# Opening the block of engine programs without GpSimd's closing drain

## The chip, the cores and the metric

The kernel runs on one core of one Trainium2 chip. The core has five engines, each with a program of its own: TensorE (PE, with its weight loads shown as PEld), VectorE (DVE), ScalarE (ACT), GpSimd (POOL) and SyncE (SP). The metric is the time of one execution in microseconds (us) as the device reports it. One execution is also recorded by a profiler; its page gives a span, from the first recorded instruction of the program to the end of the last one, and a time for the same execution, which is a little more than the span because it takes in what runs around the program.

## The reference

Two independent layers read different inputs, and their outputs are laid side by side in the last dimension (2048 rows, 512 + 512 columns, bfloat16).

```python
# A: attention, 32 heads of 16, over 2048 positions
qkv = (x @ wqkv)                         # split into q, k, v per head
p = softmax(q @ k.T * 16 ** -0.5)
a = (p @ v) @ wo
# B: gated long convolution, per channel
kv = shift_conv(k, shift_k) * v          # 4 taps
y = causal_conv(kv, ssm_k) + kv * ssm_D  # 2048 taps; written with FFTs
b = q * y
out = concatenate([a, b], axis=-1)
```

## The kernel before

The kernel is written as five lists of instructions, one for each engine. While the lists are made, a planner in Python keeps a clock for each engine and decides by its estimates which piece of work is put next on which engine. Nothing of that planner remains at run time: each instruction has at most a few semaphore waits before it and raises its engine's semaphore after it (`Eng.op` and `Eng.run`).

Attention is cut into 32 groups (a block of 128 feature columns, a block of 512 queries, and the even or the odd heads in it), and each group into blocks of 128 keys by 512 queries of one head. A step makes scores of several blocks on TensorE (line 829), takes their exponential on ScalarE, two or three PSUM banks at a time (line 856), or for some blocks in four passes on VectorE (lines 892, 918, 923, 927), and multiplies the result with V on TensorE (line 966). The output projection with `wo` (line 1141) follows for each 128 rows. Its result is copied out of PSUM by VectorE into `OUTA` (line 1149, `op_out`), and GpSimd starts the store of it to the output. The long convolution is done as matrix products with shifted copies of the filter (line 1236). These copies are read from a scratch tensor in memory by transfers that SyncE starts, and the work is fitted into the gaps of attention on TensorE.

Every transfer is made by one helper, `dma`, so that all of them carry line 369 in the profile. GpSimd starts the ones that rearrange queries (`QT<-QS`), that load and store the rows of `QN` for the second layer, the load of `wo`, and the stores of `OUTA`. SyncE starts nearly all others, and ScalarE three. Each transfer raises a semaphore when it lands.

The end is written out by hand. The last 128 rows of the projection are copied out in two halves at once, by ScalarE (line 1570) and VectorE (line 1568), into a free part of `QT`, and ScalarE and SyncE each start the store of one half (`d_outE`). Then SyncE waits for the landing of every store of the output, those that GpSimd started among them:

```python
for ds in d_outA + d_outB + [d_outE]:
    sp.op(lambda e, ds=ds: e.wait_ge(ds.sem, ds.n), inc=False)   # line 1573
```

After that the lists are put out inside one block, `with nc.Block() as block:` (line 1575): `pool.run`, `sp.run`, `pe.run`, `act.run` and `dve.run`. When the block closes, each engine gets a DRAIN, which holds the engine until its older instructions are complete, and then all engines meet in a barrier made of two semaphores, 96 and 97 in this program. The DRAINs of TensorE, VectorE, ScalarE and SyncE raise semaphore 96. GpSimd does its own DRAIN, then waits for semaphore 96, and raises semaphore 97, on which the other four wait. All of these carry line 1575 in the profile. The same form of barrier, with line 1611, stands in front of the program, before any transfer.

Of the kernel before, what the change touches and what calls it, by code (L numbers as in the profile page):

```python
# [274 lines left out]
def bass_concat_heads__mha_block__ssm_conv_h3__prompt_kernel(  # L275
# [1296 lines left out]
    for ds in d_outA + d_outB + [d_outE]:  # L1572
        sp.op(lambda e, ds=ds: e.wait_ge(ds.sem, ds.n), inc=False)

    with nc.Block() as block:
        @block.gpsimd
        def _(e):
            pool.run(e)

        @block.sync  # L1580
        def _(e):
            sp.run(e)

        @block.tensor
        def _(e):
            pe.run(e)

        @block.scalar
        def _(e):
            act.run(e)  # L1590

        @block.vector
        def _(e):
            dve.run(e)
# [31 lines left out]
```

## Time and profile before

| | us |
|---|---|
| median of 3 runs | 752.24 (751.03 to 752.8) |
| the profiled execution, its own time | 749.93 |
| its span | 748.2 |
| busy: ACT, PE, DVE, POOL | 724.6, 701.8, 701.3, 98.6 |

The profiled execution's time is 1.73 us over its span, and 2.31 us below the median of the runs. The clock granted to TensorE was 0.997 of full speed over the span.

Rows are read like this. In the view of a source line, each row is an engine and an operation with its count, then the shortest, median and longest duration in ns, then the start of the first and of the last one in us from the start of the span. An engine's name with a q behind it (POOLq, SPq) stands for that engine's sequencer: what it does there is not counted as busy. In the timeline a row begins with the start and the summed time in us, and ends with the idle time before it in brackets, with what ended it. In the view of stretches, each stretch has its length and then the busy time of each engine with its count of instructions.

### The profile page before, as it was taken

The page shows a single profiled execution, that of the slowest core. Times are in us where ns is not written, and L with a number is a line of the kernel's source. Part 1 is how long each engine was busy: PE and PEld are TensorE (multiplying, and loading weights), DVE is VectorE, ACT ScalarE, POOL GpSimd, SP SyncE. Part 2 cuts the span into 40 slices and gives each one's busy share as a digit, 9 for nine tenths or more (in the row PEclk, how much of TensorE's full clock was granted, in tenths as well). Part 3 has the DMA queues.
Part 4 walks back from the last instruction along what each step waited for, and adds up shares of the span by engine and source line. Part 5 has one row for each costly group of instructions (what it writes and reads, how often), then busy time and mean ns, then how long its engine had stood idle before and what let it go on. Part 6 is the DMA issues. An engine that isn't in the chain of part 4 may idle for free.

```text
span 748.2 us, 32527 instructions
## 1 busy us (share of the span) xinstructions
PE 701.8 (94%) x14696; PEld 315.0 (42%) x14696; DVE 701.3 (94%) x1437; ACT 724.6 (97%) x690; POOL 98.6 (13%) x172
## 2 busy tenths in 40 slices
PE   8999899999999999999999999999899999999996
PEld 3334244445443454444444444444343443434353
DVE  3999999999999999999899998999999997989993
ACT  6999999999999999999999999999899999999995
POOL 7202102020202002020021302020011201210000
PEclk9999999999999999999999999999999999999999
DMA  9698757777785777776677578666787575766110
GB/s 217 185 238 285 226 181 226 254 251 239 237 256 180 256 278 234 259 231 225 171 235 227 179 233 274 207 208 222 257 294 254 179 238 187 246 223 224 55 31 30
DMA packets 73720, 161.48 MB, mean 216 GB/s; under 512 B 34064, under 2 KB 37776, under 8 KB 73200
## 3 DMA queue, kind: packets, MB, share of 16 engines
q1 hardware_dynamic: 66400, 150.43, 62.8%
q0 software_dynamic: 5984, 8.66, 3.9%
q8 instruction: 116, 1.90, 1.0%
q10 hardware_dynamic: 1200, 0.33, 0.2%
q14 instruction: 20, 0.16, 0.1%
HBM read 142.61 MB, written 6.42 MB: 199 GB/s over the span
## 4 chain that ended last, share of the span: by engine, by line
ACT 59%; DVE 23%; PE 13%; DMA 3%; issue 1%; POOLq 0%; POOL 0%; SPq 0%
ACT PT L856 59%; DVE PTD L892 10%; PE PS L829 4%; DVE PTD L923 4%; PE PS L966 4%; DVE PTD L918 2%; DVE PTD L927 2%; DMA WR<-kz_scratch 2%; PE PS L1236 2%; PE PS L516 1%; DVE DT L1064 1%; PE PS L1493 1%; DMA xT<-in_A_x_dram 1%; DVE KV L604 1%; DVE VA L621 0%
## 5 line engine op out<-in xcount | busy, mean ns | idle before, releaser
L856 ACT ACTIVATE PT<-PS 128x1024 bf16<-128x1024 f32 (+2 forms) x686 | 722.3, 1287 | 8.6 <-PE PS L829 8.3
L892 DVE TENSOR_SCALAR PTD<-PS 128x512 uint16<-128x512 f32 x464 | 312.1, 687 | 15.0 <-PE PS L829 14.2
L829 PE MATMUL PS<-QT,KTo 32*128 32x512 bf16 (+2 forms) x2248 | 271.0, 366 | 24.4 <-ACT PT L856 14.5
L1236 PE MATMUL PS<-WR,KV 128*24 128x128 bf16 (+8 forms) x8192 | 180.8, 220 | 2.6 <-DMA WR<-kz_scratch 1.9
L966 PE MATMUL PS<-PT,VA 128*32 128x512 bf16 (+2 forms) x1748 | 180.4, 367 | 2.7 <-DVE VA L621 1.3
L1236 PEld LDWEIGHTS PS<-WR,KV 128*32 128x32 bf16 (+7 forms) x8192 | 134.5, 95 | 59.0 <-issue 33.7
L923 DVE TENSOR_TENSOR PTD<-PTD 128x1024 f16<-128x1024 f16 x232 | 156.5, 686 | 0.3
L966 PE MATMUL PS<-PTD,VA 128*32 128x512 f16 (+1 forms) x1000 | 151.8, 368 | 0.5 <-DVE PTD L927 0.4
L829 PEld LDWEIGHTS PS<-QT,KTo 32*128 32x128 bf16 x2248 | 71.2, 91 | 192.2 <-ACT PT L856 138.7
L369 POOL DMA_DIRECT2D QT<-QS x120 | 61.1, 516 | 396.1 <-DVE QS L582 372.2
L927 DVE TENSOR_SCALAR PTD<-PTD 128x1024 uint16<-128x1024 uint16 x232 | 96.5, 422 | 0.3
L918 DVE TENSOR_SCALAR PTD<-PTD 128x1024 uint16<-128x1024 uint16 x232 | 93.6, 422 | 0.3
L966 PEld LDWEIGHTS PS<-PT,VA 128*32 128x32 bf16 x1748 | 45.6, 94 | 88.2 <-issue 69.3
L966 PEld LDWEIGHTS PS<-PTD,VA 128*32 128x32 bf16 x1000 | 38.7, 95 | 12.8 <-issue 2.2
L1487 PE MATMUL PS<-IDN,ZW 128*32 128x512 bf16 (+3 forms) x178 | 42.6, 307 | 0.3 <-DVE DT L1064 0.2
L369 POOL DMA_DIRECT2D out_dram<-OUTA x15 | 8.8, 584 | 107.1 <-DVE OUTA L1149 107.1
L1064 DVE STREAM_TRANSPOSE DT<-PS 128x512 f32<-128x512 f32 x31 | 22.1, 714 | 0.4 <-PE PS L966 0.2
L570 PE MATMUL PS<-WKV,xT 128*128 128x128 bf16 x256 | 19.3, 220 | 1.1 <-DVE KTo L591 0.5
L516 PE MATMUL PS<-xT,WQ 128*32 128x512 bf16 x240 | 18.3, 384 | 1.2 <-DVE DT L1064 0.8
L516 PE MATMUL PS<-xT,WKV 128*32 128x512 bf16 (+1 forms) x256 | 18.4, 381 | 1.0 <-DVE QN L1271 0.5
L1487 PEld LDWEIGHTS PS<-IDN,ZW 128*32 128x32 bf16 x178 | 13.2, 95 | 12.7 <-issue 8.4
L570 PEld LDWEIGHTS PS<-WKV,xT 128*128 128x128 bf16 x256 | 14.4, 98 | 8.8 <-issue 3.8
(72 smaller groups left out, 250.0 us busy)
## 6 DMA issues: line engine op xcount, KB each, us to landing
WR<-kz_scratch SPq DMA_DIRECT2D x256, 512.0 KB, 5.4
KV<-KV SPq DMA_DIRECT2D x16, 256.0 KB, 5.6
kz_scratch<-WR SPq DMA_DIRECT2D x1, 2176.0 KB, 8.3
QN<-in_B_q_dram POOLq DMA_DIRECT2D x8, 256.0 KB, 5.0
out_dram<-QN POOLq DMA_DIRECT2D x8, 256.0 KB, 2.9
QT<-QS POOLq DMA_DIRECT2D x120, 16.0 KB, 4.3
out_dram<-OUTA POOLq DMA_DIRECT2D x15, 128.0 KB, 2.5
QN<-in_B_ssm_k_dram SPq DMA_DIRECT2D x1, 1024.0 KB, 8.2
```

The lines of the kernel that those rows point to most:

```text
L369: f(outp, inp).then_inc(dsem.sem, 16)
L516: ins = e.matmul(dst[g:g + 32], lhsT=w[:, g:g + 32], rhs=rhs, tile_position=(0, g), **kw)
L570: ins = e.matmul(PS[:, bank, 128 * j:128 * j + 128], lhsT=xT[:, dc, (4 * sc + j) * 128:(4 * sc + j + 1) * 128], rhs=WV[:, dc, o * 128:(o + ...
L829: ins = e.matmul(PS[:, bank, i * w:i * w + w], lhsT=KTo[32 * s:32 * s + 32, OF[n_] % 2, kt * 128:(kt + 1) * 128], rhs=QT[32 * s:32 * s + 3 ...
L856: h = act.op(lambda e: e.activation(PT[:, p0:p0 + n, :], src, ACT.Exp, scale=EXP_SCALE, bias=EXP_BIAS), [h, free], us=(0.065 + 0.4257 * n, ...
L892: h_f = urgent(lambda e: e.tensor_scalar(fix_u, PS[:, bank, :], FIX_ADD, FIX_HI, ALU.add, ALU.min), [h, h_ptd.get(i - R_PTD)], slack=S_FX)
L918: st["h"] = dve.op(lambda e: e.tensor_scalar(mant_u, fix_u, MANT, HALF_BITS, ALU.bitwise_and, ALU.bitwise_or), [st["h"]], us=us)
L923: st["h"] = dve.op(lambda e: e.tensor_tensor(mant, fix, mant, ALU.mult), [st["h"]], us=us)
L927: h = dve.op(lambda e: e.tensor_scalar(fix_u, fix_u, OCTAVE, ONE_MORE, ALU.bitwise_and, ALU.bitwise_or), [st["h"]], us=us)
L966: ins = e.matmul(dst, lhsT=w, rhs=rhs, start=first, stop=last, tile_position=(0, 32 * s))
L1236: ins = e.matmul(PS[32 * g:32 * g + 2 * ((30 - d) // 2 + 1), BGB, 128 * kk:128 * kk + w], lhsT=kv, rhs=WR[:, r + g, S - 64 * d - 128:S - 6 ...
L1487: pe.op(lambda e, s=s, k=k, rhs=rhs, bank=bank, rows=rows, c0=c0, first=first: e.matmul(PS[32 * s:32 * s + rows, bank, c0:c0 + 128 * k], l ...
```

## The change

The block is opened with an option that leaves GpSimd's DRAIN out of its closing. The other four engines still drain, and the barrier that follows is made of semaphore instructions alone: it holds GpSimd until the four have arrived, as before, but GpSimd comes to it without having drained. The five lists of instructions themselves, their waits, and the waits of SyncE for the stores are as before. Nothing that is computed changes.

```diff
     for ds in d_outA + d_outB + [d_outE]:
         sp.op(lambda e, ds=ds: e.wait_ge(ds.sem, ds.n), inc=False)
 
-    with nc.Block() as block:
+    with nc.Block(no_gpsimd_drain=True) as block:
         @block.gpsimd
         def _(e):
             pool.run(e)
```

## The prediction, made before the result was known

> **What bounds the kernel now.** I read the page first. ScalarE, TensorE and VectorE are each busy over 93% of the span, and GpSimd 13%.
>
> ```profile
> span 748.2 us, 32527 instructions
> ...
> PE 701.8 (94%) x14696; PEld 315.0 (42%) x14696; DVE 701.3 (94%) x1437; ACT 724.6 (97%) x690; POOL 98.6 (13%) x172
> ```
>
> So for most of the span the exponentials on ScalarE set the pace, with two other engines close behind. The edit touches none of that. It touches only what is recorded under line 1575, so the view that decides is the one of that source line.
>
> ```profile
> L1575 POOLq EVENT_SEMAPHORE  x2: 17/17/17, 748.0 to 748.1; - x2
> L1575 PEldq DRAIN  x1: 878/878/878, 740.6 to 740.6; - x1
> L1575 POOLq DRAIN  x1: 6514/6514/6514, 741.4 to 741.4; - x1
> L1575 DVEq DRAIN  x1: 464/464/464, 741.5 to 741.5; - x1
> L1575 ACTq DRAIN  x1: 153/153/153, 742.3 to 742.3; - x1
> L1575 SPq COMPARE_BRANCH  x1: 41/41/41, 744.0 to 744.0; - x1
> L1575 SPq DRAIN  x1: 13/13/13, 744.2 to 744.2; - x1
> L1575 SPq EVENT_SEMAPHORE  x1: 17/17/17, 748.1 to 748.1; - x1
> L1575 ACTq EVENT_SEMAPHORE  x1: 17/17/17, 748.1 to 748.1; - x1
> L1575 PEldq EVENT_SEMAPHORE  x1: 51/51/51, 748.1 to 748.1; - x1
> L1575 DVEq EVENT_SEMAPHORE  x1: 21/21/21, 748.1 to 748.1; - x1
> ```
>
> GpSimd's DRAIN takes 6514 ns, from 741.4 to about 748.0. Four engines have finished theirs at 741.5 (TensorE: 740.6 plus 0.88), 742.0 (VectorE), 742.5 (ScalarE) and 744.2 (SyncE). GpSimd's two semaphore instructions, which close the barrier, come only at 748.0 and 748.1, and all others leave right after. The second view to read is that of busy time in stretches, to see whether anything at all runs beside the long DRAIN.
>
> ```profile
> 738.00:742.00 4.00, 3.33 (x50) 1.77 (x38) 2.03 (x6) 1.35 (x3) 0.77 (x2) 1.00 0.10 35
> 742.00:744.30 2.30, 0.00 (x0) 0.00 (x0) 0.00 (x0) 0.00 (x0) 0.01 (x1) 1.00 0.36 114
> 744.30:748.20 3.90, 0.00 (x0) 0.00 (x0) 0.00 (x0) 0.00 (x0) 0.00 (x0) 0.82 0.00 0
> ```
>
> The columns after the length are PE, PEld, DVE, ACT, POOL, then clock, DMA share and GB/s. From 742.0 to 744.3 only transfers run. From 744.3 to 748.2 nothing runs: no engine, and the DMA share is 0.00. The last 3.9 us of the span are the DRAIN and the barrier alone.
>
> The third view is the timeline of the last transfers, with their times to landing and SyncE's waits.
>
> ```profile
> 741.47 0.54 POOL L369 DMA_DIRECT2D out_dram<-OUTA  x1 [3.23 <-DVE OUTA L1149]
> ...
> 741.93 0.37 ACTq L369 DMA_DIRECT2D out_dram<-QT  x1
> 741.97 0.36 SPq L369 DMA_DIRECT2D out_dram<-QT  x1
> ```
>
> ```profile
> out_dram<-OUTA POOLq DMA_DIRECT2D x2, 128.0 KB, 2.0
> out_dram<-QT ACTq DMA_DIRECT2D x1, 64.0 KB, 1.9
> out_dram<-QT SPq DMA_DIRECT2D x1, 64.0 KB, 2.0
> ```
>
> ```profile
> SPq L1575 <- PEq L1575: 3.9, 1, 3.9
> SPq L1573 <- DMA out_dram<-OUTA: 1.1, 1, 1.1
> SPq L1573 <- DMA out_dram<-QT: 0.4, 1, 0.4
> ```
>
> GpSimd's last store starts at 741.47 and lands 2.0 us later, at about 743.5; SyncE's own, at 741.97, lands at about 744.0. SyncE has waited for both before its DRAIN at 744.2, and then waits 3.9 us in the barrier. The releaser that the view names there, TensorE's DRAIN, was done at 741.5; the one that was really missing is GpSimd, by the source rows above.
>
> **The change part by part.** First, the DRAIN of 6514 ns goes. Its first part, to 744.2, lies beside the last stores and SyncE's waits and is worth nothing; that cover remains. Only what lies behind SyncE's DRAIN is on the path: from 744.2 to the barrier's first instruction on GpSimd at 748.0, 3.8 us.
>
> Second, the closing barrier stays. Its price is read from both barriers of the trace. The closing one goes from 748.0 to the end of the span at 748.2, 0.2 us. The opening one, from line 1611, is alike:
>
> ```profile
> L1611 POOLq EVENT_SEMAPHORE  x2: 17/17/17, 0.6 to 0.7; - x2
> ...
> L1611 POOLq DRAIN  x1: 179/179/179, 0.4 to 0.4; - x1
> ...
> L1611 PEldq EVENT_SEMAPHORE  x1: 51/51/51, 0.7 to 0.7; - x1
> ```
>
> It runs from 0.6 to about 0.75, again 0.2 us at the rounding of the rows. So the new program ends 0.2 us behind SyncE.
>
> Third, a plain drain followed by a semaphore instruction stands where a DRAIN raised the semaphore itself. That is one added instruction on each of four engines, 17 to 51 ns by the EVENT_SEMAPHORE rows. Only SyncE's is on the path, since the others arrive 1.7 us or more earlier. I take 0.05 us, between 0.02 (its row alone) and 0.1 (with a raise that has to travel, as between GpSimd's two rows).
>
> Fourth, what is late next: the store of the last half tile by SyncE, at 741.97 with its 2.0 us. GpSimd's store of `OUTA` is still waited for, by SyncE, so the end cannot come before about 744.0 plus the branch and DRAIN of SyncE.
>
> The new span is then 744.2 + 0.05 + 0.2 = 744.45, against 748.2: 3.75 us less, 3.7 rounded down.
>
> Fifth, the price that the trace does not show: whether something around the program has to do what the DRAIN did. The profiled execution took 749.93, which is 1.73 us more than its span, and no row tells what lies there. Two bounds follow from the rows. The least is nothing: if no one asks GpSimd again, the whole 3.7 us are gained. The most is the whole work over again. GpSimd was free for its DRAIN at 742.0 (741.47 + 0.54) and done at 748.0, so the work takes at most 6.0 us. Begun at about 744.4 instead of 742.0, it would end at 750.4, 2.4 us later than now, of which the 0.2 us of the barrier, already done, come off: a loss of 2.2 us. I take nothing. The nearest row for a drain with no transfers before it is the opening one, 179 ns, and it stands behind four small memsets that it also has to outlast; a closing sequence that only tidies up is nearer to that row than to 6 us.
>
> What makes the DRAIN long is a reason for care. Both stores of that time have landed by 744.0, yet it goes on for 4 us. Waiting for a landing is therefore not what fills it. A candidate is a charge for each transfer that GpSimd has started:
>
> ```profile
> QN<-in_B_q_dram POOLq DMA_DIRECT2D x8, 256.0 KB, 5.0
> out_dram<-QN POOLq DMA_DIRECT2D x8, 256.0 KB, 2.9
> QT<-QS POOLq DMA_DIRECT2D x120, 16.0 KB, 4.3
> out_dram<-OUTA POOLq DMA_DIRECT2D x15, 128.0 KB, 2.5
> ...
> WKV<-in_A_wo_dram POOLq DMA_DIRECT2D x1, 512.0 KB, 4.3
> ```
>
> That is 152 transfers, and 6.0 us by 152 is 39 ns for each. This is an estimate from these rows; the opening DRAIN, with no transfer behind it, fits it. If it holds, the work exists whenever someone settles those entries, and the question is only whether anyone inside the measured time does.
>
> [...]
>
> **The sum.** 749.93 - 3.7 = 746.2 for an execution like the profiled one. That execution was 2.31 us below the median of the runs, and I assume that the difference stays: 752.24 - 3.7 = 748.5, or 0.5% less.
>
> **The rivals.**
> - *Part of the work returns.* What closes the execution drops the 152 entries without waiting for each. Anything between the bounds is possible; at a quarter to a half of the 39 ns it is 1.5 to 3 us, and the time is 750.0 to 751.5, say 750.7. [...] Against it: 1.73 us around the span leave little room for long sequences.
> - *The work goes on by itself and ends when it ended.* If the DRAIN only watches something that GpSimd finishes at 748.0 in any case, and something later waits for it, the span shrinks by 3.75 us and the time by no more than the barrier's 0.2: 752.0. For it: the work starts with the last store. Against it: nothing is seen running after 744.3, though the inside of GpSimd has no rows.
> - *The work starts over later.* A drain outside the program does it all from 744.4 on. This ends on the other side: 2.2 us lost, 754.4. It decides only if that drain takes more than the 3.7 us gained; at 39 ns that is 95 of the 152 entries. For it: the estimate by count needs work and not time. Against it: someone must wait there for the same completions that the block was asked not to wait for.
> - *The option has no effect on GpSimd's DRAIN.* Then the time stays at 752.2. Against it: the option is for this DRAIN.
>
> **How the numbers follow.** Chances: the full gain 0.57; part returns 0.12; ends as before 0.10; starts over 0.18; no effect 0.03. No change is what lies within 0.2%, 1.5 us, about what a measurement of this kernel can tell. The full gain (748.5) and nearly all of the partial one (up to 750.7) are faster: 0.57 + 0.11 = 0.68. Starting over is slower: 0.18. The rest, 0.14, is the same. The three runs spread 1.2 below and 0.6 above their median, so the full gain's own range is 747.3 to 749.3. The range for 8 in 10 must also take in the partial return and the two cases near 752, and leaves out starting over: 747.0, with 0.3 us for a barrier slightly cheaper than taken, to 752.6.
>
> **What would show it.** In the new profile the row of POOLq DRAIN under line 1575 is gone, SyncE's drain stays near 744.2, GpSimd's first semaphore instruction comes at 744.3 and the span is near 744.5. The stretch with nothing in it shrinks from 3.9 to 0.3 us, and everything before 741 is alike. The span alone does not prove the gain: what counts is the execution's time over the span. At 1.7 us the full gain is right; at 3 to 5 us part of the work returned; at 5.3 us it ended as before; at over 7 us it started over. The prediction is wrong if that difference grows, or if GpSimd comes to the barrier late for another reason, such as its last store, which would show as a landing behind 744.0.

## The result, and the profile after

| | before | changed |
|---|---|---|
| median of 15 runs, us | 752.86 (750.01 to 760.29) | 746.43 (742.88 to 751.59) |
| ratio to before | | 0.9944, 95% interval 0.9922 to 0.9966 |
| the profiled execution: time, span | 749.93, 748.2 | 750.88, 749.1 |

The changed kernel is faster by 0.56%, 0.34 to 0.78%. That is 2.6 to 5.9 us of 752.86, and the 3.7 us of the forecast lie in it. The ratio is not that of the two medians, which are 6.4 us apart: single runs lie up to 10.3 us apart before and 8.7 in the changed kernel. The median of 746.43 lies 2.1 us under the forecast of 748.5 and 0.6 under its range of 747.0 to 752.6. The ratio, put on the 752.24 from which the forecast started, gives 748.0, inside the range.

The profiled execution of the changed kernel seems to contradict this: its span is 0.9 us longer than before. The closing has to be read by itself. First its source line, with engine, count, durations in ns and first and last start in us, in the changed kernel:

```profile
L1575 PEldq EVENT_SEMAPHORE  x2: 51/51/51, 746.2 to 749.0; - x2
L1575 DVEq EVENT_SEMAPHORE  x2: 21/21/21, 746.6 to 749.0; - x2
L1575 ACTq EVENT_SEMAPHORE  x2: 17/17/17, 747.1 to 749.0; - x2
L1575 SPq EVENT_SEMAPHORE  x2: 17/17/17, 748.9 to 749.0; - x2
L1575 POOLq EVENT_SEMAPHORE  x2: 17/17/17, 748.9 to 749.0; - x2
L1575 PEldq DRAIN  x1: 877/877/877, 745.2 to 745.2; - x1
L1575 DVEq DRAIN  x1: 464/464/464, 746.1 to 746.1; - x1
L1575 ACTq DRAIN  x1: 163/163/163, 746.9 to 746.9; - x1
L1575 SPq COMPARE_BRANCH  x1: 41/41/41, 748.6 to 748.6; - x1
L1575 SPq DRAIN  x1: 13/13/13, 748.8 to 748.8; - x1
```

GpSimd has no DRAIN any more. Four engines have a second semaphore instruction, the added one, and SyncE's is followed at once by GpSimd's. The span ends 0.3 us behind SyncE's DRAIN; before it was 4.0 us. Next the stretches of the end (busy time by engine, then clock, DMA share and GB/s), the last engine work, the last transfers and the barrier:

```profile
742.60:746.60 4.00, 3.31 (x50) 1.76 (x35) 2.03 (x6) 1.34 (x3) 0.77 (x2) 1.00 0.10 35
746.60:748.90 2.30, 0.00 (x0) 0.00 (x0) 0.00 (x0) 0.00 (x0) 0.00 (x0) 1.00 0.36 114
748.90:749.10 0.20, 0.00 (x0) 0.00 (x0) 0.00 (x0) 0.00 (x0) 0.00 (x0) 1.00 0.00 0
```

The first two stretches are those of before, 4.6 us later: the same 2.03 us of VectorE, and the same DMA share of 0.36 in 2.3 us in which transfers alone run. The third, with nothing in it, has shrunk from 3.9 to 0.2 us. SyncE's waits say the same:

```profile
SPq L1573 <- DMA out_dram<-OUTA: 1.1, 1, 1.1
SPq L1573 <- DMA out_dram<-QT: 0.4, 1, 0.4
SPq L1575 <- PEq L1575: 0.2, 1, 0.2
```

The wait in the barrier is 0.2 us instead of 3.9. And the anchor that both traces share, GpSimd's last store, starts 4.6 us later than before:

```profile
746.06 0.54 POOL L369 DMA_DIRECT2D out_dram<-OUTA  x1 [3.23 <-DVE OUTA L1149]
```

Starts and ends to 0.01 us, here and below, are read from the trace. From this start to the end of the span it is 749.09 - 746.06 = 3.03 us, against 748.19 - 741.47 = 6.72 before: 3.69 us less. The 4.6 us that hide it are lost long before the closing. The programs of the five engines are the same there, instruction for instruction. The exponentials' row, of before and then of the changed kernel (busy us and mean ns, then idle time before them and what ended it):

```profile
L856 ACT ACTIVATE PT<-PS 128x1024 bf16<-128x1024 f32 (+2 forms) x686 | 722.3, 1287 | 8.6 <-PE PS L829 8.3
```

```profile
L856 ACT ACTIVATE PT<-PS 128x1024 bf16<-128x1024 f32 (+2 forms) x686 | 722.6, 1290 | 13.4 <-PE PS L829 13.0
```

```profile
core 0: 749.1 us, clock 0.991
```

ScalarE worked as long as before (722.6 us against 722.3) but waited 4.8 us more, 4.7 of it for the score products of TensorE, whose granted clock was 0.991 in this execution and 0.997 in that of before. Ahead of the closing, the trace of before has one stretch of 3.41 us at half clock, at 91.4 us. The changed one has the like of it at 90.5, and three more (the clock, 0.50, stands behind the five engines):

```profile
213.36:216.77 3.41, 3.41 (x66) 1.30 (x51) 2.01 (x4) 2.01 (x2) 0.00 (x0) 0.50 0.42 91
581.99:585.40 3.41, 3.41 (x50) 1.42 (x47) 2.76 (x7) 2.59 (x4) 0.00 (x0) 0.50 0.00 0
650.26:653.67 3.41, 3.41 (x39) 0.90 (x36) 1.72 (x3) 2.05 (x2) 0.00 (x0) 0.50 0.26 89
```

TensorE is busy in all of each. Counted exponential by exponential against before, the program falls back by 2.7, 1.4 and 2.5 us across these three, and is 2.0 us ahead for the rest. That is where the 4.6 us went. In the 3.41 us just ahead of the three, TensorE was busy for only 1.49, 2.16 and 1.60; whether that is what lowers the clock was not tried. The granted clock differs between executions of one kernel, in the 15 runs of the changed one from 0.990 to 1.0: the seven with 0.998 or more have a median of 745.7, the eight below 0.996 have one of 750.2. So one profiled execution against another can't tell 3.7 us in the span; it can in the closing.

Last, the time over the span, which the forecast named as what decides: 750.88 - 749.09 = 1.79 us, before 749.93 - 748.19 = 1.74. The DRAIN's 3.7 us have not come back outside the program in this execution. Of the 15 runs of the changed kernel 13 show the same 1.7 to 1.8 us, but two show 2.2 and 2.3; none of the 46 runs of the kernel before that were made beside the experiments does.

### The profile page after: what moved, and what is told of

The parts are those of the page before. It is cut to its first block, busy times and chain, and to the rows that moved or that the text cites. A ratio compares the mean times of both kernels' runs of the same rounds, so it can differ in the third digit from the quotient of the medians.

```text
span 749.1 us, 32530 instructions
## 1 busy us (share of the span) xinstructions
PE 703.4 (94%) x14696; PEld 315.4 (42%) x14696; DVE 702.0 (94%) x1437; ACT 724.8 (97%) x690; POOL 98.7 (13%) x172
## 4 chain that ended last, share of the span: by engine, by line
ACT 60%; DVE 27%; PE 11%; issue 1%; DMA 1%; POOL 0%
ACT PT L856 60%; DVE PTD L892 11%; DVE PTD L923 5%; PE PS L829 4%; PE PS L966 4%; DVE PTD L918 3%; DVE PTD L927 3%; PE PS L1236 2%; DVE DT L1064 1%; DMA xT<-in_A_x_dram 1%; PE PS L516 1%; DVE KV L604 1%; PE PS L1493 1%; DVE OUTA L1149 1%; DVE QN L1271 0%
## 5 line engine op out<-in xcount | busy, mean ns | idle before, releaser
L856 ACT ACTIVATE PT<-PS 128x1024 bf16<-128x1024 f32 (+2 forms) x686 | 722.6, 1290 | 13.4 <-PE PS L829 13.0
L1236 PEld LDWEIGHTS PS<-WR,KV 128*32 128x32 bf16 (+7 forms) x8192 | 136.0, 95 | 58.7 <-issue 36.0
L923 DVE TENSOR_TENSOR PTD<-PTD 128x1024 f16<-128x1024 f16 x232 | 154.9, 678 | 0.3
L927 DVE TENSOR_SCALAR PTD<-PTD 128x1024 uint16<-128x1024 uint16 x232 | 94.8, 414 | 0.3
L918 DVE TENSOR_SCALAR PTD<-PTD 128x1024 uint16<-128x1024 uint16 x232 | 92.2, 415 | 0.3
L966 PEld LDWEIGHTS PS<-PTD,VA 128*32 128x32 bf16 x1000 | 38.6, 95 | 12.5 <-issue 1.6
```

The source lines that it names most:

```text
L856: h = act.op(lambda e: e.activation(PT[:, p0:p0 + n, :], src, ACT.Exp, scale=EXP_SCALE, bias=EXP_BIAS), [h, free], us=(0.065 + 0.4257 * n, ...
L918: st["h"] = dve.op(lambda e: e.tensor_scalar(mant_u, fix_u, MANT, HALF_BITS, ALU.bitwise_and, ALU.bitwise_or), [st["h"]], us=us)
L923: st["h"] = dve.op(lambda e: e.tensor_tensor(mant, fix, mant, ALU.mult), [st["h"]], us=us)
L927: h = dve.op(lambda e: e.tensor_scalar(fix_u, fix_u, OCTAVE, ONE_MORE, ALU.bitwise_and, ALU.bitwise_or), [st["h"]], us=us)
L966: ins = e.matmul(dst, lhsT=w, rhs=rhs, start=first, stop=last, tile_position=(0, 32 * s))
L1236: ins = e.matmul(PS[32 * g:32 * g + 2 * ((30 - d) // 2 + 1), BGB, 128 * kk:128 * kk + w], lhsT=kv, rhs=WR[:, r + g, S - 64 * d - 128:S - 6 ...
```

## The experiments

The theory: GpSimd's DRAIN works through the transfers that GpSimd has started and that have not been settled, at a price for each, only inside a DRAIN, and nobody else in the measured time does that work. "Settled" stands for what the DRAIN's time shows: a transfer that the next DRAIN no longer takes time for. The rivals: a fixed price behind the last landing; work that GpSimd ends by itself at its own time; a price by bytes or rows.

**One DRAIN early, the closing one kept.** The same end without the option: GpSimd drains once where it is idle anyway.

```diff
+    n_dma, ops = 0, []
+    for w, fn, sm in pool.ops:
+        ops.append((w, fn, sm))
+        n_dma += fn.__name__ == "fn"
+        if fn.__name__ == "fn" and n_dma == 149:
+            ops.append(([], lambda e: e.drain(), None))
+    pool.ops[:] = ops
     with nc.Block() as block:
```

> The closing DRAIN of GpSimd stays; one more DRAIN is put on GpSimd right after its 149th transfer, at about 716 us, ahead of 18.8 us in which it only waits. By a charge for each transfer not yet settled (39 ns), the early DRAIN takes about 5.8 us where nothing waits for GpSimd, and the closing one has 3 transfers left: it ends with the landing of the last store, some 2.1 to 2.3 us after that store was issued, ahead of SyncE. The wait of SyncE in the barrier is 0.2 us instead of 3.9 and the time is that of the changed kernel, 3.7 us (0.5%) below before. By a fixed charge behind the last landing (4 to 4.5 us whatever the count), the closing DRAIN stays at 6 to 6.5 us, the wait in the barrier at 3.8 and the time at that of before.

Ratio to before 0.9936 (0.9907 to 0.9965). The early DRAIN in its source line, and the closing one in its own, eight lines further down than before:

```profile
L1580 POOLq DRAIN  x1: 6783/6783/6783, 715.1 to 715.1; - x1
...
L1583 POOLq DRAIN  x1: 2212/2212/2212, 741.6 to 741.6; - x1
...
L1583 SPq DRAIN  x1: 13/13/13, 744.3 to 744.3; - x1
```

The long DRAIN has moved to 715, beside other work, and the closing one, with three transfers left, is over at 743.8, ahead of SyncE. It is recorded from 741.6, 0.02 us before the last store, which lands at 743.62, so its 2.2 us are that store's issue and landing: with three transfers left, this DRAIN lasted until 0.2 us behind the last landing. The gain is the same as with the option. A fixed price behind the last landing is out.

**One DRAIN late.** The changed kernel, with GpSimd waiting for all stores of the output and then draining.

```diff
+    for ds in d_outA + d_outB + [d_outE]:
+        pool.op(lambda e, ds=ds: e.wait_ge(ds.sem, ds.n), inc=False)
+    pool.op(lambda e: e.drain(), inc=False)
     with nc.Block(no_gpsimd_drain=True) as block:
```

> The changed kernel, with GpSimd made to wait for the landing of all stores of the output, as SyncE does, and then to do one DRAIN, about 2.5 us after the issue of its last store. By a charge for each transfer, worked off only inside a DRAIN, it takes the whole 152 x 39 ns = 5.9 us from there, so that the span ends 5.5 to 6 us later behind the last store than in the changed kernel, and 1.7 to 2.2 us later than before: slower than before by 0.2 to 0.3%. By work that GpSimd finishes on its own 6.5 us after its last store, it takes at most 4.0 us and the end is that of before. By a wait for landings alone it takes under 0.3 us.

Ratio 1.0023 (0.9988 to 1.0058): not faster than before, and not told apart from it by the time. The trace tells more:

```profile
L1577 POOLq DRAIN  x1: 5944/5944/5944, 746.4 to 746.4; - x1
```

GpSimd's last store started at 743.76 in this run, and all stores of the output had landed when the DRAIN began at 746.4. Most transfers were hundreds of us old, and it still takes 5.9 us. Work that ends at its own time would have been done 3.9 us after that start, 6.5 us behind the last store. The span ends 8.78 us behind the last store (752.54 - 743.76), 2.06 us more than before. So a DRAIN asked for later does all the work from there, as the third rival of the forecast had it; in the changed kernel, whose time is 1.79 us over its span, no one asks.

**32 transfers more, before the closing DRAIN.**

```diff
+    pad, d_pad = sb("PAD", [128, 256]), DmaSem(sem("d_pad"))
...
+        if fn.__name__ == "fn" and n_dma == 149:
+            for i in range(32):
+                r0, c0 = 16 * (i % 8), 64 * (i // 8)
+                d_pad.add()
+                ops.append(([], lambda e, r0=r0, c0=c0: e.dma_start(
+                    pad[r0:r0 + 16, c0:c0 + 64], QS[r0:r0 + 16, c0:c0 + 64]).then_inc(d_pad.sem, 16), None))
...
+    sp.op(lambda e: e.wait_ge(d_pad.sem, d_pad.n), inc=False)
```

> The kernel before, with 32 small transfers more on GpSimd (16 partitions x 128 bytes, into a tensor that nothing else uses), after its 149th, all landed 2 us or more before its last stores. By a charge for each transfer, the closing DRAIN is longer by 32 x 39 ns = 1.25 us: 7.7 us. By a charge by bytes or by descriptors, it is longer by less than 0.3 us; by a fixed charge it stays at 6.5 us.

```profile
L1589 POOLq DRAIN  x1: 9127/9127/9127, 744.2 to 744.2; - x1
```

9127 against 6514 ns: 2613 ns more, which is 82 ns for each of the 32. There is a price for each transfer, and it is twice my estimate. (The one time of this run, 755.29 us, is a single execution.)

**Five DRAINs along the way.** The changed kernel with a DRAIN before the 53rd, 77th, 93rd, 118th and 146th transfer of GpSimd, behind that transfer's own wait.

```diff
...
+        if fn.__name__ == "fn" and n_dma in (52, 76, 92, 117, 145):
+            ops.append((w, lambda e: e.drain(), None))
+            w = []
+        ops.append((w, fn, sm))
...
```

> The changed kernel, with five DRAINs on GpSimd, each right before a transfer and behind that transfer's wait, when everything earlier has landed long ago. Between them lie 52, 24, 16, 25 and 28 transfers. By 39 ns for each they take 2.0, 0.9, 0.6, 1.0 and 1.1 us. By a charge for each row or descriptor the fifth, with 12 stores of 128 rows among its 28, takes several times the second, whose 24 have 16 rows each. By a fixed charge all five are alike.

The same source line asked in five windows:

```profile
L1578 POOLq DRAIN  x1: 4311/4311/4311, 294.2 to 294.2; - x1
L1578 POOLq DRAIN  x1: 2002/2002/2002, 404.7 to 404.7; - x1
L1578 POOLq DRAIN  x1: 1352/1352/1352, 465.1 to 465.1; - x1
L1578 POOLq DRAIN  x1: 2083/2083/2083, 572.8 to 572.8; - x1
L1578 POOLq DRAIN  x1: 2324/2324/2324, 711.2 to 711.2; - x1
```

By 52, 24, 16, 25 and 28 transfers that is 83, 83, 84.5, 83 and 83 ns each, or 82.2 ns for each and 37 ns for the DRAIN itself. The fifth, with 12 stores of 128 KB among its 28, is as cheap for each (83.0 ns) as the second (83.4), whose 24 move 16 KB: between 16 and 128 KB no price by size shows. But 152 transfers at this price would be 12.5 us, and the late DRAIN took 5944 ns, which is 72. Where did the other 80 go?

**One DRAIN at a chosen place.** Four kernels, each the changed one with a single DRAIN as above, behind 92, 117, 129 and 141 transfers. The edit is shown against the kernel with five.

```diff
-        if fn.__name__ == "fn" and n_dma in (52, 76, 92, 117, 145):
+        if fn.__name__ == "fn" and n_dma == 92:
```

> The changed kernel, with one DRAIN on GpSimd behind 92 transfers, long after they landed. The five DRAINs lie on 82 ns for each transfer and 40 ns; by that rate the DRAIN before, with 152 transfers behind it, settled only 72, so that 80 must have been settled earlier in another way. If that happened before the 92nd, this DRAIN takes 12 x 82 ns + 40 ns = 1.0 us; if not, 92 x 82 ns + 40 ns = 7.6 us. If at most 72 are ever kept, it takes 5.9 us.

> The same, with the one DRAIN behind 117 transfers. 37 x 82 ns + 40 ns = 3.1 us if 80 have been settled by then, 117 x 82 ns + 40 ns = 9.7 us if not, 5.9 us if at most 72 are kept.

> The changed kernel, with the one DRAIN behind 129 transfers. None had been settled at 117, 80 at 149. If all are still there, 129 x 82 ns + 40 ns = 10.6 us; if 80 are gone, 49 x 82 ns + 40 ns = 4.1 us; something between, if they go a few at a time from the 118th on.

> The same behind 141 transfers: 11.6 us if all are still there, 5.1 us (61 x 82 ns + 40 ns) if 80 are gone, something between if they go a few at a time.

The DRAIN behind 92, then in one fence for each run behind 117, 129 and 141:

```profile
L1578 POOLq DRAIN  x1: 7577/7577/7577, 459.9 to 459.9; - x1
```

```profile
L1578 POOLq DRAIN  x1: 9619/9619/9619, 567.3 to 567.3; - x1
```

```profile
L1578 POOLq DRAIN  x1: 4066/4066/4066, 619.9 to 619.9; - x1
```

```profile
L1578 POOLq DRAIN  x1: 5046/5046/5046, 662.6 to 662.6; - x1
```

At 82.2 ns and 37 ns these are 92, 117, 49 and 61 transfers. All are still there at 117, and 80 are gone at 129, at 141 and at the end. They are gone at 149 as well: the early DRAIN begins under the last two issues, which end at 716.14, and from there to its end at 721.85 it is 5.71 us, 69 transfers. So the 80 go between the 118th and the 129th transfer, in one step or in a few, and without a DRAIN of the program: "only inside a DRAIN", in the theory above, does not hold for them. What sets that time was not tried. (The kernels with DRAINs along the way ran once each, 746.11 to 754.11 us, which says nothing of their speed.)

**GpSimd waits in SyncE's place.** An attempt at a still shorter closing: the waits for the stores are put on the engine that leads the barrier. Beside it ran the changed kernel once more.

```diff
     for ds in d_outA + d_outB + [d_outE]:
-        sp.op(lambda e, ds=ds: e.wait_ge(ds.sem, ds.n), inc=False)
+        pool.op(lambda e, ds=ds: e.wait_ge(ds.sem, ds.n), inc=False)
```

> The changed kernel, with the waits for the landing of the output's stores moved from SyncE to GpSimd, which leads the barrier. SyncE's branch and DRAIN behind the last landing leave the path; GpSimd has its waits, and no DRAIN, in their place. By the rows of the late DRAIN's run, GpSimd is free 0.27 us before SyncE's raise reaches it: 0.2 to 0.3 us off the end, which the trace can show and the time can't. If GpSimd takes as long as SyncE from the landing to the barrier, nothing changes.

> The changed kernel once more, beside the one above. By all theories left, 0.3 to 0.7% below before, a time 1.7 to 1.9 us over its span, and the end of the span 2.9 to 3.1 us behind the start of GpSimd's last store.

Ratios to before 0.9948 (0.9923 to 0.9973) and, for the changed kernel again, 0.9955 (0.9924 to 0.9986). From GpSimd's last store to the end of the span it is 749.51 - 746.56 = 2.95 us, against 3.02 in the repeat (747.86 - 744.84): 0.07 us instead of the 0.27 expected. The reason is in the closing's rows with GpSimd's waits:

```profile
L1575 POOLq EVENT_SEMAPHORE  x2: 17/17/17, 749.3 to 749.4; - x2
...
L1575 POOLq COMPARE_BRANCH  x1: 38/38/38, 749.1 to 749.1; - x1
```

The branch out of the list, with 0.2 us to the next instruction, which SyncE had, GpSimd now has. The time over the span, though, is 2.4 us in this profiled execution and 2.1 to 2.4 in all 12 runs, against 1.7 to 1.8 in 11 of the 12 runs of the repeat (2.4 in one). The late DRAIN's ten runs, where GpSimd ends with the same waits, show 2.2 to 2.4 as well. So 0.07 us are gained in the program and about 0.5 us lost around it. The cause of the 0.5 us is not in the rows. This is no better version.

## Why the prediction was right

- *The place* was right: only what lies behind SyncE's DRAIN was gained. The stretch with nothing in it went from 3.9 to 0.2 us and SyncE's wait in the barrier from 3.9 to 0.2. The last 4 us of work ahead of it kept their form but came 4.6 us later, for the clock, so the places named in advance, SyncE's drain near 744.2 and an end near 744.5, were met only from the common anchor on.
- *The size* was right by the trace: 3.69 us behind the common anchor, for 3.75 worked out. The barrier cost its 0.2 us, and the added semaphore instruction some 0.07: from SyncE's DRAIN to the end it is 0.30 us in the changed kernel (748.79 to 749.09) and 0.23 with the early DRAIN and the old barrier (744.335 to 744.561). The term was 0.05, between 0.02 and 0.1.
- *What is late next* was right: the end now follows the landing of SyncE's half tile, and GpSimd's store is not late.
- *The unknown price around the program* was taken as nothing: 1.74 us over the span before, 1.79 after. This was a choice more than a derivation, and lucky in part. It rested on the opening DRAIN of 179 ns, which has no transfers behind it; the late DRAIN, asked for 2.6 us behind the start of the last store, took 5.9 us, and nothing in the rows of before told that no such DRAIN would follow the block. With it fall the first rival (1.5 to 3 us return), the second (ends as before) and the fourth (no effect). A small return is left: 2.2 to 2.4 us over the span in 3 of the 27 runs of the changed kernel, two here and one in the repeat. In the early and the late DRAIN the work stood where it was asked for, so the second rival's mechanism is out as well.
- *The third rival* had the mechanism right and its condition not met: a DRAIN asked for later does start over. The late DRAIN's 5.9 us bear out the bound of 6.0, and its end, 2.06 us behind that of before, the 2.2 us of loss. No row shows what runs around the program, but the 1.79 us over the span leave no room for a DRAIN that takes 5.9 us.
- *The estimate of 39 ns* was wrong in size: it spread 6.0 us over all 152 transfers. A transfer costs 82 ns, and 72 were left. The sum did not use it. The chance of the third rival did: 95 transfers were said to make it decide; at 82 ns it takes 45.
- *The chance of a gain* was added up too high: the partial return, priced at 750.0 to 751.5 around 750.7, has only about half of its range below 750.7, so some 0.06 of its 0.12 counts as faster, where 0.11 was added.
- *The median* came out lower than forecast, 746.43 for 748.5, while the closings in the traces differ by 3.7 us. Medians of 12 runs against 23 differ by 4.9 us in the repeat (747.32 and 752.24) and by 3.9 with the early DRAIN (747.73 and 751.66). No run shows a second cause, and single runs of the changed kernel spread from 742.88 to 751.59; that the rest is spread is likely and not shown.

## What to carry to other kernels

The closing barrier was on the path here because one engine came to it late, GpSimd at 748.0 against 744.2 for SyncE, and the source line of the block shows which. GpSimd's DRAIN took 82 ns for each transfer that GpSimd had started and not settled, also for those started over 500 us before (the DRAIN behind 117 transfers, at 567.3, found none settled); with three transfers left it lasted 2.2 us, to the landing of the last. Since SyncE already waits for every store, it could be left out, or asked for earlier in a gap; the early DRAIN gained as much (0.64% against 0.56%), with 1.7 to 1.8 us over the span in all 12 runs. When a change lies wholly in the closing, compare from an anchor that both traces share, since the times of one program differ by more than the gain: by 8.7 us over the 15 runs of the changed kernel, for 3.7 gained.

## What the runs showed that was not expected

Of 152 transfers, 80 were settled between the 118th and the 129th, where a DRAIN would have paid 80 x 82 ns = 6.6 us. The helper's line in the changed kernel, asked for that stretch on GpSimd:

```profile
L369 POOL DMA_DIRECT2D QT<-QS x8: 484/490/929, 588.7 to 593.8; - x8
L369 POOL DMA_DIRECT2D out_dram<-OUTA x4: 539/550/836, 568.3 to 574.8; - x4
```

The twelve transfer instructions take 0.48 to 0.93 us each, so none of them holds such a price. Whether GpSimd pays it while it waits, 13.4 us before the first of the eight, no row can show.

And waits for the stores at the end of GpSimd's list came with some 0.5 us more around the program in every run of the two kernels that have them (2.1 to 2.4 us), whether the program ended 0.07 us earlier than the changed one or, with the late DRAIN, 5.75 us later behind the last store. The same half microsecond shows now and then where the option is used without such waits: in 3 of 27 runs of the changed kernel and in the one run with five DRAINs, but in none of the four with a single DRAIN along the way. It shows in none of the 46 runs of before and none of the 12 with the early DRAIN, which both keep the closing DRAIN. Its cause is open.
